# Block means of v from tiles of 256 positions: an add on GpSimd for every product, and half as many products

## The chip, the cores and the metric

The kernel runs on one core of a Trainium2 chip. The core has a matrix engine (TensorE, PE in the profile, with PEld for its weight loads), VectorE (DVE), ScalarE (ACT), GpSimd (POOL), and SyncE (SP), whose queue issues the DMA transfers. Each engine works through its own list of instructions in order; semaphores make one wait for another. The metric is the device time of one execution in microseconds (us), lower is better.

## The reference

Three layers follow one another: a windowed attention with 2 batches, 8 heads, 768 positions and 64 values per head, and two feed-forward layers of 512 x 2048 with different activations.

```python
block, window = (32, 16)
k_sum = k.reshape(B, H, nb, block, D).max(axis=3)
v_sum = v.reshape(B, H, nb, block, D).mean(axis=3)
scores_l = scale * (q @ k^T), kept where |i - j| < window
scores_s = scale * (q @ k_sum^T) + log(block)
a = softmax(concat(scores_l, scores_s))
attn = a @ concat(v, v_sum)
h = x @ w_in ; g = activation(h) ; x = g @ w_out      # twice
```

`v_sum` is what the change is about: for each batch the means of v over 24 blocks of 32 positions, for all 512 columns (8 heads of 64).

## The kernel before, in words

**The attention** takes 64 queries at a time (QS), so there are 24 such pieces n, 12 per batch. The keys of a piece are 96 positions around it and the 24 block rows, 120 in all (KEYS). A piece passes through a chain spread over several steps t of one loop: copy keys (`k`), scores (`qk`, tile s, L403), mask, row minimum, exponential, sum, reciprocal, normalisation (`norm`, L453), transposes on TensorE (`turn`, tile pt, L459), products with the values (`pv`, tile po, L473), and the split of the result into two float parts (xh, xl).

**The feed-forward layers** are computed in the same loop as soon as 256 or 512 rows are there: `H` (L197) gives tile h in twelve products, the activation follows on ScalarE and VectorE, `gh` and `gl` split it, and `Y` (L260) multiplies by the second weight matrix into four accumulators, again twelve products. The weights come as raw words, of which `low`, `hi`, `mid`, `end` make high and low parts; `mid` and `end` are subtractions of 128x512 (L175), in most steps on GpSimd.

**The block means.** Each 128 positions of v are loaded as one tile vt of 128 x 512 (`att_vload`, L351). `att_vmean` (L356) multiplies it with the matrix `mean` and adds into an accumulator vps in rows 96 to 119; with 6 tiles per batch there are 12 such products, each two passes on TensorE in the trace. `mean` is a wide matrix of zeros with four columns of 1/32 in 32 rows each; the slice from z0 places the four blocks of tile i in the right rows. After the last tile of a batch ScalarE copies the rows out (L368), and copies of them go behind the values of each piece.

**The order** is written out by hand. For each step t one of six strings in `ORDERS` says in which order the parts are issued; an instruction goes to the end of its engine's list at that moment, and nothing reorders the lists afterwards. `VMEAN_AT` says in which step each of the 12 products is issued:

```python
VMEAN_AT = (-1, -1, 0, 0, 1, 2, 6, 7, 8, 9, 9, 9)
VLOAD_T = 4
```

So the first batch's six stand in steps -1 to 2, the second batch's in steps 6 to 9. A step of the loop takes about 4 to 5 us there. The place of `vmean` in its string decides what is queued ahead of it: in steps 5 and 6 it stands behind `guard` and ahead of `norm` and `H`; in steps 7 to 9 behind `end`, `gl` and `pv` and ahead of `turn` and `guard`. The buffers of vt are four (NVT); a new tile is loaded into a buffer when its product has been issued, and SyncE's queue waits there until it is done. `FIRST` is the order of the loads before the loop. `keep_busy` issues products whose result nobody reads, in steps 3 to 6.

Of the kernel before, what the change touches and what calls it, by code (L numbers as in the profile page):

```python
# [9 lines left out]
F32 = mybir.dt.float32  # L10
# [7 lines left out]
ALU = mybir.AluOpType  # L18
# [3 lines left out]
P = 128  # L22
WINDOW = 16
BLOCK = 32
# [7 lines left out]
N_FIRST = 3  # L32
EARLY = 8

VMEAN_AT = (-1, -1, 0, 0, 1, 2, 6, 7, 8, 9, 9, 9)
VLOAD_T = 4
KMAX_AT = (6, 6, 6, 7, 9, 9, 9, 10)
KLOAD_AT = (4, 7)
# [15 lines left out]
     "low guard ks Y end H norm"),  # L54
)

FIRST = 'k0 v0 v1 k1 q0 q2 v2 v3 q1'

SOFTMAX = 'aaaassasaasssabssssssass'

# [12 lines left out]
def kernel(  # L73
# [14 lines left out]
    nc = tc.nc  # L88
    B, _, NPAIR, S = kT.shape
    S -= 2 * WINDOW  # L90
    NT, DM = out.shape
    NF = alpha.shape[1]
    NC = DM // P
    NB = S // BLOCK
    KEYS = STRIP + NB
# [205 lines left out]
    e1 = att_e.enter_context(tc.tile_pool(name="e1", bufs=1, side="right"))  # L301

    ident = a1.tile([P, P], F32, name="ident")
    make_identity(nc, ident)
    NQZ, NVC, NVT = 3, 4, 4
    vlate = []
    HALF = S // 2 + 2 * WINDOW
    HSUB = NSUB // 2
    NV = S // P
    bias = []  # L310
    for e in range(3):
        t = a1.tile([P, KEYS], F32, name=f"bias{e}")
        nc.gpsimd.memset(t, 0.0)
        for h2 in range(2):
            s = t[h2 * QS:(h2 + 1) * QS, 0:STRIP]
            nc.gpsimd.affine_select(out=s, in_=s, compare_op=ALU.is_gt, fill=1e9,
                                    base=0, pattern=[[1, STRIP]], channel_multiplier=-1)
            nc.gpsimd.affine_select(out=s, in_=s, compare_op=ALU.is_gt, fill=1e9,
                                    base=2 * WINDOW, pattern=[[-1, STRIP]], channel_multiplier=1)
# [6 lines left out]
    qz = [b1.tile([P, NPAIR, 2 * QS], F32, name=f"qz{i}") for i in range(NQZ)]  # L326
    kc = [b1.tile([P, NPAIR, KEYS], F32, name=f"kc{i}") for i in range(NKC)]
    vc = [a1.tile([KEYS, DM], F32, name=f"vc{i}") for i in range(NVC)]
    mean = e1.tile([P, KEYS + NB - P // BLOCK], F32, name="mean")
    nc.gpsimd.memset(mean, 0.0)  # L330
    for i in range(P // BLOCK):
        c0 = KEYS - P // BLOCK + i
        nc.gpsimd.memset(mean[i * BLOCK:(i + 1) * BLOCK, c0:c0 + 1], 1.0 / BLOCK)
    kt, kmax, vt, vmean, st = {}, {}, {}, {}, {}

    def att_load(b, half):
        pool = e1 if (b, half) == (0, 1) else ktp
        kt[b, half] = pool.tile([P, NPAIR, HALF], F32, tag="kt", name="kt")
        for hp in range(NPAIR):
            nc.sync.dma_start(out=kt[b, half][:, hp, :], in_=kT[b, :, hp, half * (S // 2):half * (S // 2) + HALF])  # L340

    def att_kmax(b, i):
        half, hp = divmod(i, NPAIR)
        if i == 0:
            kmax[b] = a2.tile([P, NPAIR, NB], F32, tag="kmax", name="kmax")
        nc.vector.tensor_reduce(
            out=kmax[b][:, hp, half * NB // 2:(half + 1) * NB // 2],
            in_=kt[b, half][:, hp, WINDOW:WINDOW + S // 2].rearrange("p (n i) -> p n i", i=BLOCK),
            axis=AX.X, op=ALU.max)

    def att_vload(b, i):  # L351
        vt[b, i] = e1.tile([P, DM], F32, tag="vt", name="vt", bufs=NVT)
        s0 = WINDOW + i * P
        nc.sync.dma_start(out=vt[b, i], in_=vS[b, s0:s0 + P, :])

    def att_vmean(b, i):  # L356

        if i == 0:
            vmean[b] = psy.tile([P, 512], F32, tag=f"y{b}", name="vps")
        z0 = (NV - 1 - i) * (P // BLOCK)  # L360
        nc.tensor.matmul(out=vmean[b][0:KEYS, :], lhsT=mean[:, z0:z0 + KEYS], rhs=vt[b, i],  # L361
                         start=(i == 0), stop=(i == NV - 1))
        n = b * NV + i + NVT
        if n < B * NV:
            vlate.append(n)
        if i == NV - 1:
            ps, vmean[b] = vmean[b], (b1 if b else e1).tile([KEYS, DM], F32, tag=f"vmean{b}", name=f"vmean{b}")
            nc.scalar.copy(vmean[b][STRIP:KEYS, :], ps[STRIP:KEYS, :])  # L368
# [169 lines left out]
    def vmean_at(t):  # L538
        for i, at in enumerate(VMEAN_AT):
            if at == t:  # L540
                att_vmean(*divmod(i, NV))
        while vlate and (vlate[0] < NV or t >= VLOAD_T):
            att_vload(*divmod(vlate.pop(0), NV))
# [40 lines left out]
    with tc.manual_schedule():  # L584
        for step in FIRST.split():
            {"k": lambda i: att_load(0, i), "v": lambda i: att_vload(0, i), "q": att_in}[step[0]](int(step[1]))
        for i in range(2 * NPAIR):
            att_kmax(0, i)
        for i, at in enumerate(VMEAN_AT):
            if at == -2:  # L590
                att_vmean(*divmod(i, NV))
# [148 lines left out]
```

## Time and profile before

| | us |
|---|---|
| median of 3 runs (616.64 to 617.71) | 617.39 |
| the profiled execution | 617.73 |
| its span | 615.9 |
| TensorE busy in it | 597.7 |
| VectorE, ScalarE, GpSimd busy | 338.7, 379.9, 358.4 |

The span is the time from the first to the last instruction of the profiled execution; some 1.8 us lie around it. Durations below are of this one execution. A clock column (PEclk) gives the granted TensorE clock as a share of full speed: 1.00 is 2.4 GHz, 0.50 is 1.2 GHz. Times of matmuls in the trace overlap a little, since they are pipelined; in the chain of waits each piece is cut where the next one takes over.

### The profile page before, as it was taken

The numbers are of one execution on the slowest core, as the hardware profiler recorded it, in microseconds if no ns is written. First come the engines' busy times: TensorE is split into PE (matmuls) and PEld (weight loads), VectorE is DVE, ScalarE is ACT, GpSimd is POOL, SyncE is SP. The second block draws the span as 40 slices with busy tenths as digits, with TensorE's granted clock in tenths as the row PEclk, the third lists the DMA queues.
The fourth block names the chain that finished last, engine by engine and source line by source line (L and its number), as shares of the span: only waits on it lengthen the run. The fifth ranks groups of instructions, "written<-read, shape, count | busy, mean of one in ns | idle before, by whom it ended". The sixth has DMA issues, their size and how long they took to land.

```text
span 615.9 us, 8657 instructions
## 1 busy us (share of the span) xinstructions
PE 597.7 (97%) x3224; PEld 498.4 (81%) x3224; DVE 338.7 (55%) x494; ACT 379.9 (62%) x659; POOL 358.4 (58%) x349
## 2 busy tenths in 40 slices
PE   5989999999999999999999999999999999999996
PEld 2767989988888888888888888888888888888884
DVE  4767687753221111145555277776566666566664
ACT  1768898877443333367777467776566666566663
POOL 3467789666612222237777558776466666466662
PEclk9989999999999999999999999999999999999999
DMA  8997566525100000024555101000100000100001
GB/s 299 323 349 248 199 211 220 194 81 206 68 1 1 1 0 1 0 87 187 205 180 185 48 0 69 0 2 1 68 2 1 0 1 1 69 0 2 2 0 68
DMA packets 17129, 55.09 MB, mean 89 GB/s; under 512 B 2368, under 2 KB 4416, under 8 KB 12992
## 3 DMA queue, kind: packets, MB, share of 16 engines
q1 hardware_dynamic: 17088, 54.55, 25.2%
q8 instruction: 25, 0.41, 0.3%
q14 instruction: 16, 0.13, 0.1%
HBM read 51.39 MB, written 3.15 MB: 89 GB/s over the span
## 4 chain that ended last, share of the span: by engine, by line
PE 76%; DVE 11%; ACT 6%; DMA 3%; POOL 2%; issue 1%; SPq 1%; DVEq 0%; ACTq 0%
PE h L197 35%; PE y L260 35%; DVE tp L232 2%; PE s L403 2%; DVE tp L222 2%; DVE h L231 2%; DVE tu L230 2%; DMA kt<-in_kT 2%; ACT h L228 2%; ACT h L229 2%; DVE tp L221 1%; PE vps L361 1%; PE pt L459 1%; PE po L473 1%; DMA qz<-in_qT 1%
## 5 line engine op out<-in xcount | busy, mean ns | idle before, releaser
L197 PE MATMUL h<-xh,wih 128*128 128x512 f32 (+1 forms) x416 | 156.4, 376 | 0.5 <-DVE tp L210 0.5
L197 PE MATMUL h<-xl,wih 128*128 128x512 f32 (+1 forms) x416 | 155.4, 374 | 0.0
L197 PE MATMUL h<-xh,wil 128*128 128x512 f32 (+1 forms) x416 | 155.2, 373 | 0.0
L244 POOL TENSOR_TENSOR gl<-tp,gh 128x512 fp32r<-128x512 f32 (+1 forms) x75 | 95.2, 1270 | 80.1 <-ACT gh L139 78.6
L139 ACT ACTIVATE gh<-tp 128x512 fp32r<-128x512 f32 (+1 forms) x76 | 46.2, 608 | 91.5 <-DVE tp L232 44.6
L197 PEld LDWEIGHTS h<-xh,wih 128*128 128x128 f32 x416 | 78.7, 189 | 15.0 <-DVE tp L210 0.7
L197 PEld LDWEIGHTS h<-xl,wih 128*128 128x128 f32 x416 | 78.6, 189 | 14.0 <-issue 0.5
L197 PEld LDWEIGHTS h<-xh,wil 128*128 128x128 f32 x416 | 78.6, 189 | 13.8
L260 PE MATMUL y<-gh,woh 128*128 128x512 f32 (+1 forms) x224 | 81.9, 366 | 0.0
L260 PE MATMUL y<-gh,wol 128*128 128x512 f32 (+1 forms) x224 | 80.4, 359 | 0.0
L260 PE MATMUL y<-gl,woh 128*128 128x512 f32 (+1 forms) x224 | 80.3, 359 | 0.0
L260 PE MATMUL y<-woh,gh 128*128 128x512 f32 x192 | 74.8, 390 | 1.1 <-ACT gh L139 1.1
L165 DVE SCALAR_TENSOR_TENSOR cv<-raw,top 128x1024 int32<-128x1024 int32 x32 | 58.8, 1838 | 30.4 <-ACT top L163 23.9
L260 PE MATMUL y<-wol,gh 128*128 128x512 f32 x192 | 74.7, 389 | 0.0
L260 PE MATMUL y<-woh,gl 128*128 128x512 f32 x192 | 74.5, 389 | 0.0
L230 DVE SCALAR_TENSOR_TENSOR tu<-tu,h 128x512 f32<-128x512 f32 x48 | 33.0, 687 | 71.0 <-ACT h L229 67.5
L219 POOL TENSOR_SCALAR tu<-tv,ab 128x512 f32<-128x512 f32 x48 | 37.2, 776 | 57.9 <-ACT tv L217 57.9
L220 POOL TENSOR_TENSOR tu<-tu,tv 128x512 f32<-128x512 f32 x48 | 62.3, 1298 | 4.0
L244 POOL TENSOR_TENSOR gl<-tu,gh 128x512 fp32r<-128x512 f32 (+1 forms) x28 | 33.2, 1184 | 49.0 <-ACT gh L139 48.9
L210 DVE SCALAR_TENSOR_TENSOR tp<-h,tp 128x512 f32<-128x512 f32 (+1 forms) x28 | 17.2, 614 | 69.0 <-ACT tp L139 69.0
L228 ACT ACTIVATE h<-tu,lnb 128x512 f32<-128x512 f32 x48 | 33.2, 692 | 35.1 <-DVE tp L222 32.7
L210 DVE SCALAR_TENSOR_TENSOR tu<-h,tu 128x512 f32<-128x512 f32 (+1 forms) x28 | 17.2, 613 | 62.0 <-ACT tu L139 62.0
(83 smaller groups left out, 1066.9 us busy)
## 6 DMA issues: line engine op xcount, KB each, us to landing
raw<-in_w_in SPq DMA_DIRECT2D x16, 1024.0 KB, 4.6
raw<-in_w_out SPq DMA_DIRECT2D x16, 1024.0 KB, 4.6
qz<-in_qT SPq DMA_DIRECT2D x25, 256.0 KB, 5.2
vc<-in_vS SPq DMA_DIRECT2D x24, 192.0 KB, 5.2
kt<-in_kT SPq DMA_DIRECT2D x16, 208.0 KB, 5.0
vt<-in_vS SPq DMA_DIRECT2D x12, 256.0 KB, 5.1
out<-stage SPq DMA_DIRECT2D x12, 256.0 KB, 2.1
al<-in_alpha SPq DMA_DIRECT2D x1, 8.0 KB, 5.5
```

Of the source, the lines that this page charges most:

```text
L139: e.activation(out=out, in_=in_, func=AF.Copy, scale=1.0 if scale is None else scale)
L165: nc.vector.scalar_tensor_tensor(out=w.bitcast(I32), in0=rest, scalar=13, in1=top, op0=ALU.logical_shift_right, op1=ALU.bitwise_or)
L197: nc.tensor.matmul(out=ps, lhsT=a, rhs=b, start=(c == 0 and m == 0), stop=(c == NC - 1 and m == 2))
L210: nc.vector.scalar_tensor_tensor(out=t, in0=ps, scalar=0.0, in1=t, op0=ALU.max, op1=ALU.subtract)
L219: nc.gpsimd.tensor_scalar(out=q, in0=v, scalar1=ab[:, 1:2], scalar2=ab[:, 0:1], op0=ALU.mult, op1=ALU.add)
L220: nc.gpsimd.tensor_tensor(out=q, in0=q, in1=v, op=ALU.mult)
L222: nc.vector.scalar_tensor_tensor(out=p, in0=p, scalar=na[:, 1:2], in1=ps, op0=ALU.add, op1=ALU.mult)
L228: nc.scalar.activation(out=A, in_=q, func=AF.Ln, scale=2.0 ** -LN_SHIFT, bias=lnb)
L229: nc.scalar.activation(out=A, in_=A, func=AF.Exp, scale=-1.0, bias=exb)
L230: nc.vector.scalar_tensor_tensor(out=q, in0=q, scalar=one, in1=A, op0=ALU.add, op1=ALU.mult)
L244: (eng("gl") if (u, f) != steps[-1] else nc.vector).tensor_tensor(out=gl, in0=t, in1=gh.bitcast(F32), op=ALU.subtract)
L260: nc.tensor.matmul(out=yps[c][:, c0:c0 + n] if layer == 0 else yps[c], lhsT=a, rhs=b, start=(f == 0 and c0 == 0 and m == 0), stop=(f == NF ...
```

## The change

A tile of v now holds 256 positions, two neighbouring positions in each partition (a tile of 128 x 2 x 512, loaded by one DMA of 512 KB). GpSimd adds the two, in place, and one product takes the sum. `mean` has eight columns, each with 1/32 in 16 rows; it is made by a memset and two selections. There are three tiles and three products per batch, two buffers of vt, and the steps of the six products are written anew.

```diff
-VMEAN_AT = (-1, -1, 0, 0, 1, 2, 6, 7, 8, 9, 9, 9)
+VMEAN_AT = (-1, 0, 2, 6, 7, 9)
-FIRST = 'k0 v0 v1 k1 q0 q2 v2 v3 q1'
+FIRST = 'k0 v0 k1 q0 q2 v1 q1'
-    NQZ, NVC, NVT = 3, 4, 4
+    NQZ, NVC, NVT = 3, 4, 2
-    NV = S // P
+    NV = S // (2 * P)
-    mean = e1.tile([P, KEYS + NB - P // BLOCK], F32, name="mean")
+    VB = 2 * P // BLOCK
+    mean = e1.tile([P, KEYS + NB - VB], F32, name="mean")
     nc.gpsimd.memset(mean, 0.0)
-    for i in range(P // BLOCK):
-        c0 = KEYS - P // BLOCK + i
-        nc.gpsimd.memset(mean[i * BLOCK:(i + 1) * BLOCK, c0:c0 + 1], 1.0 / BLOCK)
+    blocks = mean[:, KEYS - VB:KEYS]
+    nc.gpsimd.memset(blocks, 1.0 / BLOCK)
+    rows = BLOCK // 2
+    nc.gpsimd.affine_select(out=blocks, in_=blocks, compare_op=ALU.is_ge, fill=0.0,
+                            base=0, pattern=[[-rows, VB]], channel_multiplier=1)
+    nc.gpsimd.affine_select(out=blocks, in_=blocks, compare_op=ALU.is_ge, fill=0.0,
+                            base=rows - 1, pattern=[[rows, VB]], channel_multiplier=-1)
...
-        vt[b, i] = e1.tile([P, DM], F32, tag="vt", name="vt", bufs=NVT)
-        s0 = WINDOW + i * P
-        nc.sync.dma_start(out=vt[b, i], in_=vS[b, s0:s0 + P, :])
+        vt[b, i] = e1.tile([P, 2, DM], F32, tag="vt", name="vt", bufs=NVT)
+        s0 = WINDOW + i * 2 * P
+        nc.sync.dma_start(out=vt[b, i], in_=vS[b, s0:s0 + 2 * P, :].rearrange("(p a) c -> p a c", a=2))
...
-        z0 = (NV - 1 - i) * (P // BLOCK)
-        nc.tensor.matmul(out=vmean[b][0:KEYS, :], lhsT=mean[:, z0:z0 + KEYS], rhs=vt[b, i],
+        z0 = (NV - 1 - i) * VB
+        v = vt[b, i]
+        nc.gpsimd.tensor_tensor(out=v[:, 0, :], in0=v[:, 0, :], in1=v[:, 1, :], op=ALU.add)
+        nc.tensor.matmul(out=vmean[b][0:KEYS, :], lhsT=mean[:, z0:z0 + KEYS], rhs=v[:, 0, :],
                          start=(i == 0), stop=(i == NV - 1))
```

What this does to the engines' lists is shown at three places; lines of the changed kernel are some 5 to 7 higher than before, and the words in brackets are the semaphores of the engines and DMA queues that a row waits for. GpSimd's list from step 5 to step 7, before (wil is the low part of a weight, d the sums of the softmax, p its probabilities):

```order
L175 TENSOR_TENSOR wil_433<-cv,wih_432 128x512 [waits Activation_49]
L445 TENSOR_SCALAR d<-d 128x4 [waits DVE_49]
L453 TENSOR_TENSOR p<-p,d 128x480 [waits Pool_49]
L175 TENSOR_TENSOR wil_433<-cv,wih_432 128x512
L175 TENSOR_TENSOR wil_481<-cv,wih_480 128x512 [waits Activation_49]
L445 TENSOR_SCALAR d<-d 128x4 [waits DVE_49]
L453 TENSOR_TENSOR p<-p,d 128x480 [waits Pool_49]
L175 TENSOR_TENSOR wil_481<-cv,wih_480 128x512
L445 TENSOR_SCALAR d<-d 128x4 [waits Activation_49]
```

And the same place now, with the adds of steps 6 and 7 (L367):

```order
L460 TENSOR_TENSOR p<-p,d 128x480 [waits Pool_49]
L175 TENSOR_TENSOR wil_422<-cv,wih_421 128x512
L175 TENSOR_TENSOR wil_470<-cv,wih_469 128x512 [waits Activation_49]
L452 TENSOR_SCALAR d<-d 128x4 [waits DVE_49]
L367 TENSOR_TENSOR vt<-vt 128x512 [waits DMAHW0_49]
L460 TENSOR_TENSOR p<-p,d 128x480 [waits Pool_49]
L175 TENSOR_TENSOR wil_470<-cv,wih_469 128x512
L367 TENSOR_TENSOR vt<-vt 128x512 [waits DMAHW1_49]
L452 TENSOR_SCALAR d<-d 128x4 [waits Activation_49]
```

The add of step 6 stands behind two weight subtractions and the guard and ahead of the normalisation; that of step 7 behind the next subtraction. On TensorE the product of step 6 keeps its place between the transposes and the `h` products, and waits for GpSimd now beside its load.

GpSimd's list in step 9, before (wol is a weight's low part, gl the low part of the activation):

```order
L453 TENSOR_TENSOR p<-p,d 128x480 [waits DVE_49]
L175 TENSOR_TENSOR wol_637<-cv,woh_636 128x512
L244 TENSOR_TENSOR gl<-tp,gh 128x256 [waits Activation_49]
L445 TENSOR_SCALAR d<-d 128x4 [waits Activation_49]
L175 TENSOR_TENSOR wol_706<-cv,woh_705 128x512 [waits Activation_49]
```

and now:

```order
L460 TENSOR_TENSOR p<-p,d 128x480 [waits DVE_49]
L175 TENSOR_TENSOR wol_626<-cv,woh_625 128x512
L244 TENSOR_TENSOR gl<-tp,gh 128x256 [waits Activation_49]
L367 TENSOR_TENSOR vt<-vt 128x512 [waits DMAHW0_49,PE_49]
L452 TENSOR_SCALAR d<-d 128x4 [waits Activation_49]
L175 TENSOR_TENSOR wol_694<-cv,woh_693 128x512 [waits Activation_49]
```

The add stands behind gl and ahead of the guard.

TensorE's list in step 9, before:

```order
L473 MATMUL po<-pT,vc_185 64x64 x7
L361 MATMUL vps<-vt,mean 120x512 [waits DMAHW6_49]
L361 MATMUL vps<-vt,mean 120x512 [waits DMAHW5_49]
L361 MATMUL vps<-vt,mean 120x512 [waits DMAHW2_49]
L459 MATMUL pt<-ident,p 120x128 [waits PE_49,Pool_49]
L459 MATMUL pt<-ident,p 120x128 x3
L260 MATMUL y_727<-gh,woh_636 128x256
```

and now:

```order
L480 MATMUL po<-pT,vc_185 64x64 x7
L368 MATMUL vps<-vt,mean 120x512 [waits DMAHW0_49,Pool_49]
L466 MATMUL pt<-ident,p 120x128 [waits PE_49]
L466 MATMUL pt<-ident,p 120x128 x3
L260 MATMUL y_714<-gh,woh_625 128x256
```

Two products are gone, and the one left waits for GpSimd (Pool); the transposes and `y` products follow it as before.

## Rows read from the trace of the kernel before

**Rows 1.** The page, busy us of each engine (share of the span, instructions).
```profile
PE 597.7 (97%) x3224; PEld 498.4 (81%) x3224; DVE 338.7 (55%) x494; ACT 379.9 (62%) x659; POOL 358.4 (58%) x349
```

**Rows 2.** Windows of 5 us from 55 to 155 us, their sum.
```profile
sum 100.00, PE 98.43 PEld 90.03 DVE 64.50 ACT 84.03 POOL 74.62; mean PE 4.92 PEld 4.50 DVE 3.23 ACT 4.20 POOL 3.73
```

**Rows 3.** Chain of waits in order of time: start, us, what; steps 0 to 2.
```profile
13.13 3.07 PE vps L361 x4
16.20 0.90 PE s L403 x8
...
20.23 0.86 PE vps L361 x2
```

**Rows 4.** The same chain in step 6.
```profile
36.91 1.71 PE vps L361 x2
38.62 1.94 PE h L197 x12
...
40.58 0.39 ACT tu L206
```

**Rows 5.** The same chain in step 9.
```profile
51.86 2.77 PE vps L361 x6
54.62 0.44 PE pt L459 x4
```

**Rows 6.** Timeline of TensorE: start, us, instruction [idle before, and its end].
```profile
11.07 2.06 PE L403 MATMUL s<-kc,qz 128*128 128x120 f32 x8 [0.44 <-POOL kc L141]
...
18.22 1.12 PE L403 MATMUL s<-kc,qz 128*128 128x120 f32 x8 [0.27 <-issue]
```

**Rows 7.** Tile vt: its loads (ns min/median/max, first and last start), time to landing.
```profile
L354 SPq DMA_DIRECT2D vt<-in_vS x12: 327/431/1387, 2.6 to 43.4; - x12
...
DMA to landing us min/median/max: 4.2/5.1/6.5
```

**Rows 8.** Timeline of all engines, 0 to 26 us, GpSimd's last preparation.
```profile
6.75 0.12 POOL L323 MEMSET bias<- 128x16 f32 x1
```

**Rows 9.** Timeline of all engines, step 8.
```profile
47.11 0.59 PEld L459 LDWEIGHTS pt<-ident,p 128*120 128x120 f32 x4 [0.44 <-POOL p L453]
```

**Rows 10.** Timeline of GpSimd, step 6.
```profile
35.88 2.50 POOL L175 TENSOR_TENSOR wil<-cv,wih 128x512 fp32r<-128x512 f32 x2
...
38.75 0.99 POOL L453 TENSOR_TENSOR p<-p,d 128x480 f32<-128x480 f32 x1
```

**Rows 11.** Tile wil, GpSimd's subtraction: ns min/median/max, first and last start.
```profile
L175 POOL TENSOR_TENSOR wil<-cv,wih x32: 1269/1294/2119, 32.5 to 379.2; 128x512 fp32r<-128x512 f32 x32
```

**Rows 12.** Windows: busy us of PE, PEld, DVE, ACT, POOL; PEclk; DMA share, GB/s.
```profile
34.00:36.00 2.00, 0.58 (x17) 0.44 (x16) 1.93 (x5) 1.26 (x3) 1.83 (x4) 1.00 1.05 432
36.00:37.00 1.00, 1.00 (x5) 1.00 (x6) 1.00 (x4) 0.00 (x0) 1.00 (x1) 0.61 0.98 387
37.00:38.00 1.00, 1.00 (x3) 0.36 (x2) 0.48 (x2) 0.60 (x1) 1.00 (x2) 0.50 1.02 416
...
39.00:40.00 1.00, 1.00 (x8) 1.00 (x7) 0.00 (x0) 1.00 (x1) 1.00 (x2) 0.69 1.01 361
```

**Rows 13.** Timeline of TensorE, the transpose of step 6.
```profile
35.98 0.93 PE L459 MATMUL pt<-ident,p 128*120 128x128 f32 x4 [1.42 <-POOL p L453]
```

**Rows 14.** Timeline of GpSimd, step 9.
```profile
52.38 0.99 POOL L453 TENSOR_TENSOR p<-p,d 128x480 f32<-128x480 f32 x1 [1.25 <-DVE d L449]
53.33 1.28 POOL L175 TENSOR_TENSOR wol<-cv,woh 128x512 fp32r<-128x512 f32 x1
54.58 0.73 POOL L244 TENSOR_TENSOR gl<-tp,gh 128x256 fp32r<-128x256 f32 x1
55.39 0.19 POOL L445 TENSOR_SCALAR d<-d 128x4 f32<-128x4 f32 x1
```

**Rows 15.** Timeline of GpSimd, its waits near steps 2 to 4 and 7.
```profile
21.84 1.17 POOL L141 COPY vc<-vmean 24x512 f32<-24x512 f32 x2 [10.62 <-ACT vmean L368]
...
43.10 0.19 POOL L445 TENSOR_SCALAR d<-d 128x4 f32<-128x4 f32 x1 [2.12 <-ACT p L433]
```

## The prediction, made before the changed kernel ran

> **What bounds the kernel now.** I began with the busy times: TensorE is busy for 597.7 of 615.9 us [rows 1], so the naive reading is that whatever leaves TensorE is gained. From 55 to 155 us it is busy for 98.43 of 100 us [rows 2]; time that TensorE loses before 55 us is therefore hardly given back later. What matters is the attention phase, and there I read the chain of waits in order of time. Its first stretch is TensorE: the scores of step 0, a pair of mean products and the scores of step 1, behind which the softmax work on VectorE begins [rows 3]. In the middle it reaches a mean product at 36.91 and a group of `h` products whose end at 40.56 releases ScalarE at 40.58 [rows 4]; the chain then passes through ScalarE and VectorE, so a late `h` moves everything. The third stretch is TensorE again: `po`, three mean products from 51.86 to 54.62, the transpose and the `y` products [rows 5]. So six of the twelve products lie where they are paid. The other question is when GpSimd, which now must add before each product, gets to its add; for that I read its own timeline around 36 to 40 and 52 to 56 us.
>
> **What is removed.** A product takes 0.86 us at the clock's upper level and 1.71 at half [rows 3, 4]. At the start, one of the pair of step 0 is gone: 3.07 / 2 = 1.54 us before the scores of step 1 [rows 3]. If these scores then still run at half clock they take 2.06 instead of 0.90, as the scores of step 0 do [rows 6], and only 0.4 is left. Were half clock to stay for the next scores and product too (1.16 and 0.85 more), 1.6 us would be lost instead. In the trace the full level was there at 16.2; the scores would begin at 14.7 and straddle that. I take a gain of 0.8, bounds -1.5 to +1.6 on the time. The first product of the pair of step -1 now waits for a double tile, an add and a select: a load lands 4.2 to 6.5 us after its issue [rows 7], the first is issued at 2.6 [rows 7], so the add starts between 6.8 and 9.1, takes 1.27, the select about 0.3 (estimated from the 0.12 of the memset it stands beside [rows 8]), the product 1.71 at half clock: done between 10.1 and 12.4. The scores of step 0 start at 11.07, released by GpSimd's copy of the key maxima [rows 6]; so 0 to 1.3 us late, taken as 0. The product of step 1 is worth nothing: behind it TensorE waits 0.27 for the next scores, whose keys VectorE copies later [rows 6]. The product of step 8 is worth nothing either: the transpose behind it waits for GpSimd's normalisation, with TensorE's weight path idle 0.44 [rows 9]. Two of three at step 9 are worth 2.77 - 0.86 = 1.91 us [rows 5], if the third can start.
>
> **What is added: a wait at step 6.** TensorE comes to its product at 36.91 [rows 4]. GpSimd is in a backlog of its own there: two weight subtractions from 35.88, the guard, and only at 38.75 the slot where the add now stands, ahead of the normalisation [rows 10]. A two-input operation of 128x512 takes 1.269 at least and 1.294 in the median, 2.119 at most [rows 11]; the add has that shape, and I take 1.27. So the product starts at 40.0 instead of 36.9: 3.1 us. The normalisation behind the add moves from 38.75 to 40.0; its reader, the transpose of step 7, is behind the delayed products anyway. Behind the product on TensorE stand the twelve `h` products; ScalarE's relu, the exponentials behind it in ScalarE's queue, GpSimd's guard and VectorE's product wait for them. On SyncE the load of the last v tile waits for this same product, and the key loads behind it move with it: taken at no extra cost, as their readers move too. Then the clock: after a thin stretch (busy 0.58 of 2 us up to 36) TensorE ran at 0.61 of full from 36 to 37, at 0.50 in each of the two microseconds after it and at 0.69 from 39 to 40 [rows 12], so 0.39 + 0.50 + 0.50 + 0.31 = 1.70 us of work lost. In the changed kernel the half level starts as before, but the wait lies inside it and the `h` products may stay slow to their end: between 0 and 1.7 more, taken 0.3. Step 6 costs 3.4 (2.8 with a GpSimd that arrives a little earlier, 4.8 at most).
>
> **The Trainium skill on this wait.** The trace shows TensorE idle 1.42 us ahead of the transpose of step 6, while the mean product, which waits for nothing but its load, stood behind it and did not pass [rows 13]. "TensorE: Matmul & The Clock Gate", Part 2, says the same and more: only weight loads are pulled ahead, "The MATMULs themselves stay in program order". If products could overtake, the two waits would cost nothing and the sum would be the removed work alone.
>
> **A wait at step 9.** Here three products become one, but it needs the add, which stands on GpSimd behind the normalisation (52.38, itself released by VectorE), a weight subtraction (53.33) and the low half of g (54.58), and ahead of the guard that starts at 55.39 [rows 14]. The add runs 55.39 to 56.66. TensorE is there at 51.86 [rows 5]: it waits 4.8 us, of which 1.91 are the removed products: 2.9 net. Queued behind it are the transpose, twelve `y` products and the next scores. All GpSimd work behind the add is 1.27 later, covered by the longer TensorE wait. And 4.8 us without a product is more than the gaps that dropped the clock at 36, so I add the 1.70 of that fall [rows 12], bounds 0 to 2.5 (one and a half times as much): 4.6 us.
>
> By the Trainium skill ("TensorE: Matmul & The Clock Gate", Part 1) half clock is the default and sustained activity releases it. By that rule the fall is all but sure: the sum would stand and rival (a) below would pass most of its chance to the forecast; I keep (a) because no row here shows one long gap in a dense stretch.
>
> The adds of steps 0, 2 and 7 cost nothing: GpSimd sits idle 10.62 us before its copy at 21.84 and 2.12 us before the guard at 43.10, and these waits hide them [rows 15]. Six adds at 1.27 are 7.6 us of GpSimd's 358, but only two stand where TensorE comes first.
>
> **The sum.** -0.8 (start) + 3.4 (step 6) + 4.6 (step 9) - 0.5 for late TensorE hiding part of the 1.57 us that it idles between 55 and 155 [rows 2] = +6.7 us. The profiled execution took 617.73 us (span 615.9 and 1.8 around it), so 624.4; it was 0.34 over the median of the three runs, 617.39, so 624.1.
>
> **Rivals.** (a) The clock does not fall at step 9, or the products at step 6 recover sooner: the same waits without 1.7, 622.4. For it: the steps before are dense. Against: less idle time brought it down at 36. (b) The start goes wrong: half clock lasts beyond step 1, or the first add comes with the late end of its load; then +1.3 to +1.6 in place of -0.8, and 626.5 (627.8 with both). For it: TensorE has half as much to do before 16 us. Against: the scores fill that place. (c) Faster: GpSimd's adds are ready when TensorE arrives and the removed work is the whole effect: 617.39 - 1.54 - 1.91 = 613.9. Its place is the two add slots, its price 3.45, and it decides when GpSimd reaches them before 35.6 and 50.6; the rows say 38.75 and 55.39, so the GpSimd queue would have to run 3 to 5 us earlier, while its releasers (ScalarE's split, VectorE's reciprocal) do not move by more than the 1.5 gained at the start. (d) No change: the wait at step 6 is absorbed by ScalarE's and VectorE's waits and the one at step 9 by the `y` work; against: ScalarE starts 0.02 us after `h` ends.
>
> **From this to numbers.** Forecast 0.55 (622.5 to 626.5), (a) 0.18, (b) 0.14, (c) 0.08, (d) 0.05. The range from 619.5 to 628.5 takes in the forecast, (a) and (b) with the bounds above, and leaves out (c) and (d). A run of this kernel can tell about 0.2%, or 1.2 us, from no change: faster 0.08, same 0.05, slower 0.87.
>
> **What would show it.** Right: in the chain or the waits, TensorE's mean product released by GpSimd's add, some 3 us near 40 us and some 4 to 5 us near 59 us; the granted clock at 0.5 behind the second; TensorE's busy time down, its span up. Wrong: the mean products released by anything but the add, waits under 1 us, or a granted clock that stays at 1.00 through step 9 (then (a)); first scores later than 11.5 us (then (b)); the first solid stretch of TensorE beginning earlier than before (then (c)).

## The result: 1.5% slower, and the profile after

| | before | after |
|---|---|---|
| median (lowest to highest), us | 617.01 (615.65 to 617.71), 4 runs | 625.57 (625.12 to 627.14), 4 runs |
| the profiled execution, us | 617.73 | 625.89 |
| its span, us | 615.9 | 624.2 |

The ratio is 1.0146, with a 95% interval from 1.0134 to 1.0158. The forecast was 624.1 with a range from 619.5 to 628.5. The sign and the mechanism were right; the sum came out too small, because the clock behind both waits was priced too low and a gain was counted that did not come.

The page's busy row of after, to be read beside [rows 1]:

```profile
PE 593.1 (95%) x3212; PEld 497.7 (80%) x3212; DVE 338.3 (54%) x494; ACT 379.8 (61%) x659; POOL 365.2 (59%) x354
```

TensorE has 12 instructions and 4.6 us less to do and the span is 8.3 us longer. So it idles more. Where, the waits of TensorE in the first 110 us of after say (engine, line and tile that waited, engine and tile waited for: us in total, times, longest):

```profile
PE vps L368 <- POOL mean L337: 9.9, 1, 9.9
PE vps L368 <- POOL vt L367: 9.0, 3, 4.7
```

The first row is the program's start. The second is new: three mean products waited 9.0 us for GpSimd's add. TensorE's timeline of after (start, us, instruction, in brackets idle time and its releaser) shows which; the scores `s` stand among them, as marks of the steps:

```profile
11.71 1.90 PE L410 MATMUL s<-kc,qz 128*128 128x120 f32 x8
14.47 1.12 PE L368 MATMUL vps<-vt,mean 128*120 128x512 f32 x2 [0.85 <-POOL vt L367]
15.42 1.05 PE L410 MATMUL s<-kc,qz 128*128 128x120 f32 x8
...
30.38 1.15 PE L410 MATMUL s<-kc,qz 128*128 128x120 f32 x8
...
39.44 2.06 PE L368 MATMUL vps<-vt,mean 128*120 128x512 f32 x2 [3.43 <-POOL vt L367]
43.86 1.23 PE L410 MATMUL s<-kc,qz 128*128 128x120 f32 x8
...
53.61 1.15 PE L410 MATMUL s<-kc,qz 128*128 128x120 f32 x8
60.07 2.06 PE L368 MATMUL vps<-vt,mean 128*120 128x512 f32 x2 [4.70 <-POOL vt L367]
```

3.43 us at step 6 and 4.70 at step 9, both released by the add (L367). The timeline of GpSimd in step 9 of after shows why the add was late; it answers to [rows 14]:

```profile
55.90 0.99 POOL L460 TENSOR_TENSOR p<-p,d 128x480 f32<-128x480 f32 x1 [1.25 <-DVE d L456]
56.84 1.28 POOL L175 TENSOR_TENSOR wol<-cv,woh 128x512 fp32r<-128x512 f32 x1
58.07 0.72 POOL L244 TENSOR_TENSOR gl<-tp,gh 128x256 fp32r<-128x256 f32 x1
58.76 1.26 POOL L367 TENSOR_TENSOR vt<-vt 128x512 f32<-128x512 f32 x1
```

The add did not wait for its data there. It waited for its turn, behind the normalisation, a weight subtraction and the low half of g. And the clock, by windows of after with the columns of [rows 12]:

```profile
36.00:38.00 2.00, 0.02 (x1) 0.00 (x0) 0.87 (x2) 0.60 (x1) 1.91 (x3) 0.85 1.03 412
38.00:40.00 2.00, 0.56 (x1) 0.48 (x2) 0.00 (x0) 1.36 (x1) 1.92 (x3) 0.50 1.01 366
...
42.00:44.00 2.00, 2.00 (x11) 2.00 (x11) 0.00 (x0) 0.00 (x0) 0.80 (x1) 0.50 0.70 218
56.00:58.00 2.00, 0.00 (x0) 0.00 (x0) 1.97 (x5) 2.00 (x7) 2.00 (x2) 0.97 0.64 184
58.00:60.00 2.00, 0.00 (x0) 0.00 (x0) 1.09 (x3) 0.30 (x1) 2.00 (x3) 0.50 0.95 389
60.00:62.00 2.00, 1.93 (x3) 0.77 (x4) 0.18 (x1) 0.00 (x0) 1.84 (x4) 0.50 1.05 309
62.00:64.00 2.00, 2.00 (x11) 2.00 (x10) 0.00 (x0) 1.55 (x3) 1.82 (x2) 0.50 0.70 203
```

TensorE had almost nothing to do from 36 to 39.4 us and nothing from 56 to 60; both times the granted clock fell to 0.50, and the next 4 us ran at 1.2 GHz. The chain of waits of after shows what that does behind the two products, to be compared with [rows 4] and [rows 5]:

```profile
38.12 1.28 POOL vt L367
39.44 2.06 PE vps L368 x2
41.50 2.56 PE h L197 x12
...
58.80 1.23 POOL vt L367
60.07 2.06 PE vps L368 x2
62.14 0.85 PE pt L466 x4
62.99 2.26 PE y L260 x12
...
71.12 1.43 PE y L260 x12
```

In step 6 the product takes 2.06 instead of 1.71 and the `h` group 2.56 instead of 1.94. In step 9 the product takes 2.06 (0.86 at the upper level), the transposes 0.85 instead of 0.44, the `y` group 2.26 (1.43 when the same chain comes to `y` again).

One table serves all that follows. TensorE's timeline gives the start of the scores of each step; the differences cut the program into stages: the start to step 6, step 6, steps 7 and 8, step 9, and all the rest of the span. One profiled execution of each kernel, in us; the last columns are the median of the timed runs (and their number) and the ratio of these runs to those of the kernel before, run beside them on the same chip (it can differ from the ratio of the medians in the fourth place). e_ stands for an experiment; after_again is the changed kernel once more.

| kernel | to s6 | 6 | 7, 8 | 9 | rest | time (runs) | ratio, 95% |
|---|---|---|---|---|---|---|---|
| before | 30.99 | 9.39 | 9.71 | 6.54 | 559.3 | 617.0 to 617.4 beside these | |
| after | 30.38 | 13.48 | 9.75 | 11.47 | 559.1 | 625.57 (4) | 1.0146 [1.0134, 1.0158] |
| after_again | 30.79 | 13.50 | 9.74 | 11.61 | 559.2 | 626.37 (4) | 1.0154 [1.0136, 1.0171] |
| e_noadd | 30.36 | 7.78 | 11.71 | 6.13 | 559.2 | 617.11 (11) | 0.9993 [0.9985, 1.0002] |
| e_noadd_warm | 31.62 | 7.77 | 10.99 | 6.53 | 559.2 | 617.23 (12) | 0.9995 [0.9983, 1.0007] |
| e_twoprod | 30.93 | 10.31 | 9.72 | 6.53 | 559.2 | 618.56 (12) | 1.0021 [1.0012, 1.0031] |
| e_add9_in8 | 32.47 | 13.49 | 9.75 | 6.53 | 559.3 | 623.08 (5) | 1.0086 [1.0074, 1.0098] |
| e_add9_again | 31.06 | 13.51 | 9.76 | 6.53 | 559.2 | 621.67 (6) | 1.0075 [1.0059, 1.0091] |
| e_busy | 29.90 | 11.48 | 9.71 | 9.44 | 559.2 | 623.42 (5) | 1.0099 [1.0084, 1.0114] |
| e_prod6_in7 | 31.58 | 6.91 | 14.45 | 10.72 | 559.1 | 623.86 (4) | 1.0108 [1.0082, 1.0135] |
| e_add6_in5 | 32.62 | 10.63 | 9.72 | 10.92 | 559.1 | 624.35 (4) | 1.0113 [1.0096, 1.0129] |
| e_both | 29.89 | 11.61 | 9.70 | 6.52 | 559.2 | 619.51 (7) | 1.0036 [1.0019, 1.0052] |
| e_best | 31.97 | 6.91 | 11.61 | 6.21 | 559.3 | 617.59 (12) | 1.0014 [0.9996, 1.0031] |
| e_dve | 37.28 | 11.18 | 11.56 | 9.51 | 559.2 | 630.73 (4) | 1.0217 [1.0192, 1.0242] |

A stage that an edit does not touch repeats within 0.06 us where no wait for an add stands in it (6.52 to 6.54 in step 9, 9.70 to 9.76 in steps 7 and 8). Two stretches do not. Step 9 with its wait takes 11.47 and 11.61 in the two profiles of the changed kernel, and 10.92 in e_add6_in5, which leaves it alone. And the start: after and e_add6_in5 issue the same work before step 5, and reach step 6 at 30.38 and 32.62. The rest is 559.1 to 559.3 for every kernel: what step 9 ends with is what the program ends with.

From before to after: -0.6 to step 6, +4.1 in step 6, 0.0 in steps 7 and 8, +4.9 in step 9, -0.2 behind; together +8.3, the difference of the spans (rounded).

### The profile page after: what moved, and what is told of

Read it like the earlier page. It is cut to its first block, busy times and chain, and to the rows that moved or that the text cites. A ratio compares the mean times of both kernels' runs of the same rounds, so it can differ in the third digit from the quotient of the medians.

```text
span 624.2 us, 8637 instructions
## 1 busy us (share of the span) xinstructions
PE 593.1 (95%) x3212; PEld 497.7 (80%) x3212; DVE 338.3 (54%) x494; ACT 379.8 (61%) x659; POOL 365.2 (59%) x354
## 4 chain that ended last, share of the span: by engine, by line
PE 75%; DVE 10%; ACT 6%; DMA 4%; POOL 3%; issue 1%; SPq 1%; DVEq 0%; ACTq 0%; POOLq 0%
PE h L197 35%; PE y L260 34%; DVE tp L232 2%; DVE tp L222 2%; DVE h L231 2%; DVE tu L230 2%; DMA kt<-in_kT 2%; PE s L410 2%; ACT h L228 2%; ACT h L229 2%; DVE tp L221 1%; PE po L480 1%; PE pt L466 1%; PE vps L368 1%; DMA vt<-in_vS 1%
```

## The experiments

The theory was that both losses come from the wait for the add in GpSimd's order, with the clock's fall behind it. The rivals: the larger loads and their two buffers; GpSimd's 7.6 us of added work as such; or the clock alone.

**No add at all** (e_noadd).

```diff
-        nc.gpsimd.tensor_tensor(out=v[:, 0, :], in0=v[:, 0, :], in1=v[:, 1, :], op=ALU.add)
```

> The changed kernel without its six GpSimd adds: each product takes the even positions alone, so half of v is left out of the means; loads, tiles, steps and the six products stay. Theory (the two products that wait for an add cost all of the 8.6 us and more): both waits go and what is left is the removed work, about 0.6 to 1.5 us at the start and 1.9 at step 9, so 613.5 to 614.5, below the kernel before (617.0). Rival A (the double loads or the new order of loads cost the time): stays above 622. Rival B (only GpSimd's 7.6 us of added work matters, wherever it stands): about 617 to 618.

617.11 us. The 8.5 us are gone, so the add is the cause; but the six removed products gain nothing, where 2.5 to 3.5 us were expected. The theory's number failed, and this run alone does not refute rival B, whose range it meets; the kernels below that keep the adds and move them do. The table shows why nothing is gained. Step 6 is 1.61 shorter than before and step 9 0.41, and steps 7 and 8 give 2.00 back. TensorE's timeline of e_noadd, columns as above:

```profile
45.83 0.65 PE L465 MATMUL pt<-ident,p 128*120 128x128 f32 x4 [1.59 <-POOL p L459]
...
54.80 0.39 PE L260 MATMUL y<-gh,woh 128*128 128x256 f32 x1 [1.34 <-ACT vmean L374]
```

and two of its windows (columns as before):

```profile
46.00:48.00 2.00, 1.36 (x8) 1.12 (x8) 1.36 (x3) 1.97 (x5) 0.60 (x1) 0.67 1.02 404
48.00:50.00 2.00, 2.00 (x11) 2.00 (x11) 2.00 (x4) 1.52 (x4) 1.48 (x2) 0.50 0.95 309
```

In step 8 the transpose waits 1.59 for the normalisation where the removed product used to stand [rows 9], and then the clock falls, in a place where it stays up in before and in after (1.00 from 46 to 52 us in both). In step 9, with two products less, the `y` group waits 1.34 for ScalarE to copy the mean accumulator out, which it must before `y` may use it.

**The new tiles and loads, two products each** (e_twoprod): twelve products again, no add.

```diff
-        nc.gpsimd.tensor_tensor(out=v[:, 0, :], in0=v[:, 0, :], in1=v[:, 1, :], op=ALU.add)
-        nc.tensor.matmul(out=vmean[b][0:KEYS, :], lhsT=mean[:, z0:z0 + KEYS], rhs=v[:, 0, :],
-                         start=(i == 0), stop=(i == NV - 1))
+        for a in range(2):
+            nc.tensor.matmul(out=vmean[b][0:KEYS, :], lhsT=mean[:, z0:z0 + KEYS], rhs=v[:, a, :],
+                             start=(i == 0 and a == 0), stop=(i == NV - 1 and a == 1))
```

> The tiles of 256 positions alone: no adds, and each tile gives two products (even and odd positions), twelve in all, in the steps of the changed kernel. Against the kernel before, a product moves from step 1 to step 2 (+0.9), a second one stands in step 6 at half clock (+1.7) and in step 7 (+0.9 at most), one less in step 9 (-0.9). Theory: 618 to 620, without any wait for GpSimd. Rival A (the loads): 622 or more.

618.56 us, ratio 1.0021, as expected. The loads are not the cause. The 0.9 us in step 6 is its second product there (in TensorE's timeline four passes take 3.40 us from 36.59, where two took 1.71 before).

**Step 9's add one step earlier** (e_add9_in8, and the same kernel as e_add9_again beside after_again). The add is taken out of `att_vmean` and issued in front of the product at the step that a second tuple names:

```diff
+VADD_AT = (-1, 0, 2, 6, 7, 8)
...
+    def att_vadd(b, i):
+        v = vt[b, i]
+        nc.gpsimd.tensor_tensor(out=v[:, 0, :], in0=v[:, 0, :], in1=v[:, 1, :], op=ALU.add)
```

> The changed kernel with one thing moved: the add for step 9's product is issued in step 8, where GpSimd waits 1.67 us for VectorE; the product stays in step 9. Theory: the 4.7 us wait at step 9 goes, and with it the half clock behind it, 4.4 to 5.0 us in all: 620.6 to 621.2; the wait of step 6 stays at 3.4. Rival B (GpSimd's added work counts wherever it stands): 625. Rival C (the clock stays low for another reason than the wait): 622.5, with the granted clock at 0.5 behind step 9 as now.

> Step 9's add issued in step 8, once more. Its first trace gained 5.0 us in step 9 but began 2.1 later, at half clock through the scores of step 1. Theory: the start is a matter of the single run, and against the changed kernel beside it this one is 3.5 to 5.0 faster (620.5 to 622.5). Rival: moving the add is worth only the 2.5 of the first medians (623).

> The changed kernel once more, beside the two that each move one add, on the same chip: 625.0 to 626.5 as before; a second profile of it shows whether the 0.6 us gained at the start holds, or whether TensorE's clock sometimes rises a group of scores later (then 1.5 to 2.5 more there).

The first time 623.08, more than the theory's range and near rival C's number, though not for its reason; the second time 621.67, in the range, against 626.37 for the unchanged kernel beside it, which came out as expected: 4.7 less. In both traces step 9 is 6.53 again, as before the change, so without its wait it is 4.9 to 5.1 shorter. What hid part of that in the first profiled execution was the start (32.47 against 31.06 in the second); of the other timed runs there is no trace. TensorE's timeline of e_add9_in8, to be compared with the rows of after at 14.47 and 15.42:

```profile
14.81 2.06 PE L372 MATMUL vps<-vt,mean 128*120 128x512 f32 x2 [0.88 <-POOL vt L364]
16.66 1.90 PE L414 MATMUL s<-kc,qz 128*128 128x120 f32 x8
```

The same instructions took 0.94 and 0.85 longer, which are their durations at half clock. The clock column can't confirm it: it reads 1.00 from the start on in before, after and e_add9_in8 alike, also where the products take 2.06, so the clock at the start is read from durations alone. Of nine profiled executions with this start three went so (e_add9_in8, e_best, e_add6_in5) and reached step 6 at 32.0 to 32.6, six not, at 29.9 to 31.6.

**Idle products in the two waits** (e_busy): TensorE multiplies something that nobody reads, 12 passes ahead of step 6's product and 32 ahead of step 9's.

```diff
-BUSY = {(3, 'pv'): 6, (4, 'pv'): 4, (5, 'qk'): 4, (6, 'qk'): 2}
+BUSY = {(3, 'pv'): 6, (4, 'pv'): 4, (5, 'qk'): 4, (6, 'qk'): 2, (6, 'turn'): 6, (9, 'pv'): 16}
```

> The changed kernel with products whose result nobody reads put into the two waits: 6 of 128x128 ahead of the mean product of step 6, 16 ahead of that of step 9. The waits themselves stay. Theory (part of each wait's cost is the half clock behind it): at step 9 product, transposes and the y group run at full clock, 1.0 + 0.4 + 0.8 = 2.2 us less; at step 6 product and h group, up to 1.0 + 1.1 less; so 620.5 to 623.5, granted clock 1.00 behind step 9. Rival (the low clock costs nothing, the wait alone does): 625 to 626.

623.42, at the upper end of the range. TensorE's timeline of e_busy, and two of its windows behind it:

```profile
38.99 1.12 PE L368 MATMUL vps<-vt,mean 128*120 128x512 f32 x2 [2.10 <-POOL vt L367]
...
52.78 3.84 PE L501 MATMUL idle<-ident 128*128 128x128 f32 x32
57.56 1.12 PE L368 MATMUL vps<-vt,mean 128*120 128x512 f32 x2 [0.94 <-POOL vt L367]
```

```profile
38.00:40.00 2.00, 1.01 (x3) 0.53 (x4) 0.00 (x0) 1.36 (x1) 2.00 (x3) 1.00 1.03 342
...
58.00:60.00 2.00, 2.00 (x14) 1.53 (x13) 0.00 (x0) 1.26 (x3) 2.00 (x2) 1.00 1.05 315
```

In the profiled execution the products start as late as in after (9.1 us after the scores of step 6, 6.5 after those of step 9, the same two intervals in both), but at the full clock, and step 6 costs 2.0 less, step 9 2.0 less. So, with the clock up, the stages are +2.1 and +2.9 against before (which itself lost some clock in step 6 [rows 12]), and the clock makes the other 4 us of the 9.0. The timed difference is only 2.2 to 3.0; the profiled execution (span 619.7) was the fastest of the five, and of the other four there is no trace. Their mean granted clock is 0.995 to 1.000, against 0.989 in all eight runs of the changed kernel, so the clock came back for the most part in all five; where the other four lost time stays open.

**Step 6 by two ways.** The product and its add one step later (e_prod6_in7), or only the add one step earlier (e_add6_in5); and the latter with step 9's add in step 8 (e_both):

```diff
-VMEAN_AT = (-1, 0, 2, 6, 7, 9)
+VADD_AT = (-1, 0, 2, 7, 7, 9)     # e_prod6_in7
+VMEAN_AT = (-1, 0, 2, 7, 7, 9)
...
+VADD_AT = (-1, 0, 2, 5, 7, 9)     # e_add6_in5, products as in the change
...
+VADD_AT = (-1, 0, 2, 5, 7, 8)     # e_both, products as in the change
```

> The changed kernel with one thing moved: the first add and product of the second batch go from step 6 to step 7, so step 7 has two of each; step 9 keeps its wait. Theory: the wait of 3.4 us at step 6 and the slow h group go (4.1), some 1.0 comes back at step 7 (a second product and up to 0.4 of waiting), and step 9 keeps its 4.4 to 5.0: 621.5 to 623. Rival (the wait of step 6 is covered by ScalarE's wait for a weight load): 625.

> The changed kernel with step 6's add issued in step 5, between guard and normalisation; its product stays in step 6 and step 9 keeps its wait. The add then delays the normalisation of step 5 and the transposes that wait for it by 1.3, but the mean product of step 6 has no wait. Theory: 3.4 + 0.7 (slow product and h) less, 1.3 more: 621.5 to 623.5 . Rival (the wait of step 6 is covered by ScalarE's wait for a weight load, 1.0 us in the trace before): 624 to 625.

> Step 6's add issued in step 5 and step 9's in step 8, all products where the changed kernel has them, nothing left out. Theory: both waits go, 1.3 comes back at step 5, and since the kernel without adds is at 617.1, this is at 617.5 to 619. Rival B (GpSimd's added work counts wherever it stands): 621 or more.

e_prod6_in7 missed its range, at 623.86: step 6 falls to 6.91, and steps 7 and 8 grow by 4.74. The wait moved along: the products of step 7 now wait 2.70 for their adds, and the clock falls behind them (last section). e_add6_in5 also missed, at 624.35, a number in its rival's range. Its stages do not speak for the rival: step 6 is 2.85 shorter than in after, where the theory had 2.8, and keeps 1.24 of its loss. The theory's total failed in this trace at the start, 32.62 against 30.38 and 30.79 in the changed kernel. The timelines of TensorE and GpSimd in e_add6_in5:

```profile
38.84 1.05 PE L470 MATMUL pt<-ident,p 128*120 128x128 f32 x4 [2.65 <-POOL p L464]
39.69 1.91 PE L372 MATMUL vps<-vt,mean 128*120 128x512 f32 x2
...
59.43 2.06 PE L372 MATMUL vps<-vt,mean 128*120 128x512 f32 x2 [4.70 <-POOL vt L364]
```

```profile
36.58 1.26 POOL L364 TENSOR_TENSOR vt<-vt 128x512 f32<-128x512 f32 x1
37.80 0.98 POOL L464 TENSOR_TENSOR p<-p,d 128x480 f32<-128x480 f32 x1
```

The product no longer waits for the add, but the transpose ahead of it waits for the normalisation that now stands behind the add: 2.65 instead of 1.42 [rows 13], and those 1.23 are nearly one add of 1.26. In step 9 the wait is 4.70, as in after, and the stage 0.55 shorter: the `y` products are at the upper level from 62.8, 3.4 us after the product begins, and in after from 64.7, 4.6 us after. e_both, 619.51, is half a microsecond above its range. In its trace the transpose of step 6 waits 3.40, since the add itself waits 0.84 for its load; step 6 keeps 2.2, step 9 nothing. Rival B, 621 or more for added work wherever it stands, is refuted.

**On VectorE** (e_dve).

```diff
-        nc.gpsimd.tensor_tensor(out=v[:, 0, :], in0=v[:, 0, :], in1=v[:, 1, :], op=ALU.add)
+        nc.vector.tensor_tensor(out=v[:, 0, :], in0=v[:, 0, :], in1=v[:, 1, :], op=ALU.add)
```

> The changed kernel with its six adds on VectorE instead of GpSimd, in the same places of the steps. VectorE takes about half the time for such an add. Theory (what counts is what stands ahead of the add in its engine's queue): step 6 has no wait, as VectorE is free from 36 us, but the first add comes behind the key maxima at 10.6 us, that of step 0 behind the mask, that of step 7 behind a minimum (some 1.9 us of wait) and that of step 9 behind one too (2.7): 621 to 626. Rival (the add's duration on GpSimd is what costs): the waits shrink everywhere, 615 to 618.

630.73, above the range. The tile's row of VectorE (ns min/median/max, first and last start) and TensorE's waits:

```profile
L367 DVE TENSOR_TENSOR vt<-vt x6: 679/727/1676, 11.2 to 63.7; 128x512 f32<-128x512 f32 x6
```

```profile
PE vps L368 <- DVE vt L367: 21.6, 6, 12.1
```

The add takes 0.73 us in place of 1.27 and yet all six products wait, 9.5 us beside the start's 12.1. "GPSIMD Engine Reference", section 4.1 of the Trainium skill sends an elementwise add to VectorE, where it is about twice as fast. This trace agrees roughly on the duration; the total went the other way, since the adds stand behind other work in VectorE's list too. The loss is at the start, which reaches step 6 6.9 us later than in after: the first add comes behind the key maxima, the second behind a mask and a minimum, and the second product takes 2.06 where after has 1.12:

```profile
18.04 2.06 PE L368 MATMUL vps<-vt,mean 128*120 128x512 f32 x2 [2.26 <-DVE vt L367]
```

The waits of steps 7 and 9, 1.77 and 3.34, are near the 1.9 and 2.7 that were expected, and steps 6 to 9 together are 2.5 shorter than in after.

**Other places for adds and products** (e_best), and **no add with TensorE kept busy in step 8** (e_noadd_warm):

```diff
-VMEAN_AT = (-1, 0, 2, 6, 7, 9)
+VADD_AT = (-1, 0, 2, 7, 7, 8)     # e_best
+VMEAN_AT = (-1, 0, 2, 7, 8, 9)
...
-BUSY = {(3, 'pv'): 6, (4, 'pv'): 4, (5, 'qk'): 4, (6, 'qk'): 2}
+BUSY = {(3, 'pv'): 6, (4, 'pv'): 4, (5, 'qk'): 4, (6, 'qk'): 2, (8, 'pv'): 6}     # e_noadd_warm
```

> Adds and products apart: the adds of the second batch are issued in steps 7, 7 and 8, where GpSimd waits for others, the products in steps 7, 8 and 9. Nothing is left out. Theory (only a product that waits for its add costs): both waits go, at most 0.4 us is left at step 7, the product of step 8 keeps TensorE from idling, and step 6 has one product less than before: 615.0 to 617.0, 8 to 10 less than the changed kernel. Rival B (GpSimd's 7.6 us of added work counts wherever it stands): 620 or more.

> The changed kernel without adds (half of v left out of the means), with 6 products of 128x128 whose result nobody reads put into step 8, where the trace of the kernel without adds shows TensorE idle 1.59 us and then twelve h products at half clock. Theory (the removed product of step 8 had kept the clock up, and that is where the gain of the removed work went): the h group takes 1.5 instead of 2.6, so 615.6 to 616.2 against 617.1. Rival (ScalarE and the weight loads set the pace there, the clock costs nothing): 617.1 as without them.

e_best, with six adds and six products, takes 617.59, slightly above its range: as fast as the kernel before within what can be told, not faster. Its theory was right in the total and wrong in one place: step 7 was to keep at most 0.4 of waiting, and its product waits 2.70 for its add there. Steps 6 to 8 take 18.52 all the same, against 19.10 before, as step 6 has one product less. By the ratios (1.0014 against 0.9993 and 0.9995) the six adds cost about 1 us against the kernels without adds, at the edge of what can be told, not 8.5: GpSimd's 7.6 us of added work is not what the change paid for.

e_noadd_warm, 617.23, missed its range and met the number of its rival, that other engines set the pace. Keeping the clock up in step 8 takes back 0.7 of the 2.0 (10.99 instead of 11.71), and step 9 loses 0.4. Four kernels leave step 6 early (7.8, 7.8, 6.9 and 6.9), and all four have steps 7 and 8 of 11 us or more: e_best and e_prod6_in7 with the wait for the add in step 7, the two kernels without adds without it. For these two, ScalarE's conversion of the raw weights in the timeline, first of before, then of e_noadd_warm, and the DMA queue of the latter from 25 to 50 us (packets, MB, share of 16 engines) show a likely reason:

```profile
38.64 1.38 ACT L163 ACTIVATE top<-raw 128x1024 f16<-128x1024 bf16 x1 [1.04 <-DMA raw<-in_w_out]
```

```profile
39.65 1.39 ACT L163 ACTIVATE top<-raw 128x1024 f16<-128x1024 bf16 x1 [1.69 <-DMA raw<-in_w_out]
```

```profile
q1 hardware_dynamic: 3264, 8.78, 102.6%
```

ScalarE has its raw weights 7.65 us after the scores of step 6 begin in before and 8.03 here; the DMA engines are full through this stretch, and an earlier `h` does not bring the load earlier. No kernel here moved these loads, so that they set the pace is argued from these rows and not shown.

## Why the prediction was right, and where its terms were off

**The waits: right, and their sizes too.** The forecast put the add of step 6 behind the backlog of [rows 10], 7.76 us after the scores of that step, and that of step 9 behind the g half of [rows 14], 5.30 after. They started 7.74 and 5.15 after. The product of step 6 began 3.1 us later in its step than before, as forecast, and the wait at step 9 was 4.70 for 4.8.

**The clock at step 6: mis-sized.** 0.3 us was taken, with a bound of 1.7. The product and the `h` group took 0.97 more than before, by the rows above, and the stage 4.1 instead of 3.4. The wait did not lie inside the half level that [rows 12] show: here that level lasted to 44 us, to the end of the `h` group.

**The clock at step 9: right in kind, 0.3 too small in this execution.** Forecast 1.7, bounds 0 to 2.5. By rows 1.20 for the product, 0.41 for the transposes and 0.83 for `y`, 2.44, of which the stage shows 2.0 (with the 2.9 of the wait, as e_busy has it: 4.9). Against the same 9.44 of e_busy, step 9 lost 2.2 in after_again and 1.5 in e_add6_in5, behind the same wait of 4.70: the 1.7 lies within what executions differ by. Rival (a) fell with this. By "TensorE: Matmul & The Clock Gate", Part 1 of the Trainium skill, the fall was to be expected, and here the trace agrees: 0.50 in the windows from 58 to 64 us.

**The start: right to 0.2 in this execution.** -0.6 for -0.8. The first scores came at 11.71, 0.6 late within the 0 to 1.3, and the forecast's sign for rival (b), scores later than 11.5, misled: the start was a gain all the same; the wait of the second product for its add (0.85, its load landing late) was not foreseen. The bound of +1.6, half clock beyond step 1, is what three of nine profiled executions show: rival (b)'s mechanism exists, and comes and goes between executions of the same start. That this one missed it is luck.

**Late absorption: wrong.** -0.5 was taken because TensorE idles 1.57 of the 100 us in [rows 2]. The windows of after, behind the waits:

```profile
70.00:155.00 85.00, 83.50 (x803) 76.93 (x802) 56.29 (x104) 71.83 (x150) 62.98 (x63) 1.00 0.53 180
```

1.5 us idle are still there. In before the same stretch, from 61.7 to 146.7 us, has TensorE busy for 83.47 of 85.00. Both have the same two waits for copies on ScalarE, 0.8 and 0.7 us: that work is later too when TensorE is, and neither wait shrank.

**The value of removed work: wrong, beside the sum.** Rival (c) priced it at 3.45 us. Without any add it was worth 0.3 (617.11 against 617.43, with an interval of the ratio that holds 1), because behind a removed product stands another wait. In the sum, the 1.91 of step 9 did count, since TensorE's own wait stood on the path there: 4.8 less 1.91 is the 2.9 that e_busy shows.

Together: 0.2 (start), 0.7 and 0.3 (clock) and 0.5 (absorption) make 1.7, which turns the forecast of +6.7 into +8.4; the span shows +8.3. All four errors had the same sign, so none hid another, and together they stayed inside the range.

## What to carry to other kernels

When an engine with slack takes over work that a busy engine must wait for, the price is not its duration but what stands ahead of it in that engine's list: read the list at each place, and put the operand a step earlier than its reader, but not ahead of work that others wait for, or it delays that by its own length. Of work removed from the busiest engine, ask at each place what that engine waits for next. Where a wait empties TensorE, allow for half the clock in the work behind it as well.

## What the runs showed that was not expected

- The same wait can leave the clock up or drop it. In step 7 both e_best and e_prod6_in7 wait 2.70 us for the add, after a stretch with little in it. The product and two windows of e_best, then of e_prod6_in7:

```profile
43.25 1.12 PE L372 MATMUL vps<-vt,mean 128*120 128x512 f32 x2 [2.70 <-POOL vt L364]
...
40.00:42.00 2.00, 0.55 (x16) 0.41 (x14) 0.03 (x1) 1.97 (x4) 2.00 (x3) 1.00 0.99 340
42.00:44.00 2.00, 0.75 (x2) 0.42 (x3) 1.86 (x4) 2.00 (x10) 2.00 (x2) 1.00 1.05 261
```

```profile
42.85 3.77 PE L372 MATMUL vps<-vt,mean 128*120 128x512 f32 x4 [2.70 <-POOL vt L364]
...
40.00:42.00 2.00, 0.16 (x6) 0.02 (x2) 0.53 (x2) 1.97 (x6) 2.00 (x3) 1.00 0.99 288
42.00:44.00 2.00, 1.15 (x2) 0.47 (x2) 1.86 (x4) 1.63 (x8) 2.00 (x2) 0.52 1.07 263
```

  One stays at 2.4 GHz; the other falls to 1.2 GHz, and its two products take 3.77 us. Why, these runs do not tell.
- The products that the change removed had also kept TensorE from idling: in e_noadd, which comes to step 8 earlier, the clock fell there, where it had stayed up before, and six products that nobody reads kept it up again in e_noadd_warm.
- The 12 timed runs of e_best lie between 616.0 and 620.5 us, and their mean granted clock (0.994 to 1.000) does not sort them. That mean can't show a slow start, as the column reads 1.00 there. What sets these runs apart stays open.
